# Value features in chunks of whole heads (six of 120 rows for five of 128), with another order of the head of the program and of the last two tiles

## The chip, the cores and the metric

The kernel runs on one core of a Trainium2 chip. The metric is device time in microseconds (us). A core has TensorE (PE) for matrix products into the eight banks of PSUM, VectorE (DVE), ScalarE (ACT) and GpSimd (POOL) for elementwise work, and SyncE (SP), whose queue issues nearly all transfers here.

## The reference, cut to what matters

```python
xn = layernorm(x)                                     # x: 2048 x 640, no scale or shift
q, k, v = split(xn @ wqkv)                            # 32 heads of 20 features
phi = lambda t: where(t > 0, t + 1, exp(t)) + 1e-6
kv  = einsum("bhsd,bhse->bhde", phi(k), v)            # 20 x 20 for each head
z   = einsum("bhsd->bhd", phi(k))
num = einsum("bhqd,bhde->bhqe", phi(q), kv)
den = einsum("bhqd,bhd->bhq", phi(q), z)[..., None] + 1e-6
s   = merge_heads(num / den) @ wo
g   = silu(relu(xn @ w1) @ w2)                        # 640 -> 1728 -> 640
out = x + s * g
```

## The kernel before

The program is a list of operations for each engine, written out by hand in one order. A small scheduler (`Sched`) derives the semaphore waits from the names that each operation reads and writes; each engine then runs its own list strictly in order. So the place of a call in the source sets what stands behind what on an engine, and a transfer that waits holds up those behind it on SP. The 2048 tokens are 16 tiles of 128 (index t), or 4 chunks of 512 (index j); the 640 features are 5 chunks of 128 (C = 5).

*Head.* Tiles 0 to 3 are the way in. For each: `LN_stats` (two halves of statistics and an aggregate on DVE, then the inverse root on POOL), `LN_norm` on DVE, `transposes` (five PE transposes into one bank), `xnT_copy` on ACT, and `K_mm`, ten passes of 320 columns in two banks (key weights from two loads, wk 0 with rows 0 to 383 and wk 1 with the rest). `K_exp` and `K_relu` on ACT empty those banks. `warm(n)` issues n products of the identity into bank 7 that nobody needs. `K_mm(t, b, ks)` with a range does only the row chunks in it. After tile 3 come, for each chunk of 512 tokens, five `Q_block` and thirteen `H_block` (the hidden layer), with statistics, norms, DMA transposes and key products of the next tiles between them.

*Fold.* After the denominators, `G_block` makes GT = xn' phi(k) over all tokens (640 x 640). `kv_block(c, b)` multiplies the value weights of chunk c (128 value features as weight columns) with the columns of GT that belong to the heads of the chunk, 140 or 160 of them, five passes for each chunk; DVE copies the result to `kvp` under a mask `mh` that keeps only each head's own features, since chunks of 128 features cut heads of 20. `kvp` is first filled with zeros by POOL (name `kvz`). `W_block(m)` multiplies `kvp` with `wo` for the 128 key features of block m, over those chunks that hold a head of the block: 2, 3, 3, 3 and 2 chunks, in two halves of 320 columns. So the attention output and its projection become one folded weight `wf` (640 x 640). Each block's two halves are copied by ACT (`wf` columns 0 to 319) and DVE (the rest), and blocks take turns between banks 4, 5 and 6, 7:

```python
        for m in range(C):
            pr[0] = 2 + m % 2
            W_block(m)
```

*Output.* `U(p, hook)` computes the second layer for a pair of tiles, in two groups of 26 passes (L771) with Silu on ACT; `hook` is called between the groups and puts other PE work there: `kv_all` in U(0), `w_all` in U(1), and then `s_tile` for the tiles of an earlier pair. `s_tile` is ten passes of `wf` (L810), then on DVE a product with g (L824), a sum with x (L827) and a store by SP. For the last pair, tiles ea and eb, the kernel before uses `s_half`: one half of each tile ahead of the last group of U(7), the other halves after it, with ea's last sum on POOL and its store issued by ACT.

Of the kernel before, what the change touches and what calls it, by code (L numbers as in the profile page):

```python
# [211 lines left out]
def bass_recurrent_scan__linear_attn_block__dense_activation_relu__prompt_kernel(  # L212
# [25 lines left out]
    x2 = A_x[0]  # L238
    out2 = out[0]

    h_lo = [(P * c) // DH for c in range(C)]
    h_hi = [-(-(P * (c + 1)) // DH) for c in range(C)]

    def cs_of_m(m):
        return [c for c in range(C) if DH * h_lo[c] < P * (m + 1) and DH * h_hi[c] > P * m]

    bf = dt.bfloat16
    f32 = dt.float32
# [10 lines left out]
    NOUT = 4  # L259
    reg3 = nc.alloc_sbuf_tensor("reg3", [P, T * D], bf)  # L260
    pk = reg3[:, :].rearrange("p (t n) -> p t n", t=T)
    kvp = reg3[:, 0:C * D].rearrange("p (c n) -> p c n", c=C)
    outb = reg3[:, C * D:(C + NOUT) * D].rearrange("p (a n) -> p a n", a=NOUT)
    tmpo = reg3[:, (C + NOUT) * D:(C + 2 * NOUT) * D].rearrange("p (a n) -> p a n", a=NOUT)
    pqT = nc.alloc_sbuf_tensor("pqT", [P, C, S], bf)
    hT = nc.alloc_sbuf_tensor("hT", [P, NF, S], bf)
    hTl = nc.alloc_sbuf_tensor("hTl", [P, 2, 512], bf)
# [12 lines left out]

    reg7 = nc.alloc_sbuf_tensor("reg7", [P, XR * D], bf)
    xin = reg7[:, :].rearrange("p (t n) -> p t n", t=XR)
    wo_sb = reg7[:, 0:C * D].rearrange("p (c n) -> p c n", c=C)

    NEK = 4
    NER = 3
# [54 lines left out]
    x_load(1)  # L341
    w_load(wqk[:, 0:KS, D:2 * D], A_wqkv[0:P * KS, D:2 * D], ("wk", 0))
    x_load(2)
    x_load(3)
    w_load(wqk[:, KS:C, D:2 * D], A_wqkv[P * KS:D, D:2 * D], ("wk", 1))

    def late_loads(gate):
        w_load(wqk[:, :, 0:D], A_wqkv[:, 0:D], ("wq",), extra=[gate])
# [18 lines left out]
        sc.group("PE", [(lambda eng: eng.matmul(ps[7][:, 0:P], lhsT=ident[:], rhs=ident[:], start=True, stop=True))  # L367
                        for _ in range(n)], R=[("ident",)], W=[("ps", 7)])

    warm(33)  # L370

    def build_consts():
        sc.op("POOL", lambda eng: eng.memset(mh[:, :, :], 1.0), W=[("mh",)])
# [61 lines left out]
    def K_mm(t, b, ks=None):  # L435
        fns = []
        for a, k in ([(a, k) for a in range(2) for k in range(C)] if ks is None else [(a, k) for k in ks for a in range(2)]):
            if True:
                fns.append(lambda eng, a=a, k=k: eng.matmul(  # L439
                    ps[b + a][:, 0:HN], lhsT=xnT[:, k, tok(t)], rhs=wqk[:, k, D + HN * a:D + HN * (a + 1)],  # L440
                    start=(k == 0), stop=(k == C - 1)))
        wks = [0, 1] if ks is None else sorted({0 if k < KS else 1 for k in ks})
        sc.group("PE", fns, R=[("xnT", t)] + [("wk", i) for i in wks], W=[("ps", b), ("ps", b + 1)])
        if ks is not None:
            sc.allow_unread.update([("ps", b), ("ps", b + 1)])
# [102 lines left out]
    LN_stat(1, 1)  # L548
    LN_aggr(1)
    LN_root_pool(1)  # L550
    LN_stat(2, 0)
    LN_norm(1)
    K_mm(0, 0, range(0, KS))
    transposes(1, 5)
    xnT_copy(1, 5)
    LN_stat(2, 1)
    LN_aggr(2)
    LN_root_pool(2)
    warm(2)
    K_mm(0, 0, range(KS, C))  # L560
    K_exp(0, 0)
    K_relu(0, 0)
    LN_stats(3)
    LN_norm(2)
    K_mm(1, 2, range(0, 4))
    transposes(2, 6)
    xnT_copy(2, 6)
    K_mm(1, 2, range(4, C))
    LN_norm(3)
    warm(3)  # L570
    transposes(3, 4)
    xnT_copy(3, 4)
    K_mm(2, 5)
    K_exp(1, 2)
    K_relu(1, 2)
    K_fin(0)
# [104 lines left out]
    for u in range(2):  # L681
        dma("SP", lambda eng, u=u: eng.dma_start(w2l[64 * u:64 * (u + 1), :], B_w2[NF * P:FF, :]),
            W=[("w2l", u)], extra=[lastW1])
    w_load(wo_sb, A_wo, ("wo",), extra=[last_norm[0]])
    for c in range(C):
        dma("SP", lambda eng, c=c: eng.dma_start(rx[:, c, :], rxd[P * c:P * (c + 1), :]),
            R=[("rxd", i) for i in range(J)], W=[("rx", c)], extra=[lastW1])
# [23 lines left out]
                                                func=ACTF.Copy), R=[("ps", b), ("ps", b + 1)], W=[("GT", k)])  # L711
        return ag

    def kv_block(c, b):
        n0, n1 = DH * h_lo[c], DH * h_hi[c]
        nh = h_hi[c] - h_lo[c]
        sc.group("PE", [(lambda eng, k=k: eng.matmul(ps[b][:, 0:n1 - n0], lhsT=wv_sb[:, k, P * c:P * (c + 1)],  # L717
                                                     rhs=GT[:, k, n0:n1], start=(k == 0), stop=(k == C - 1)))
                        for k in range(C)], R=[("wv",)] + [("GT", k) for k in range(C)], W=[("ps", b)])
        sc.op("DVE", lambda eng: eng.tensor_tensor(  # L720
            out=kvp[:, c, n0:n1].rearrange("p (h e) -> p h e", e=DH),
            in0=ps[b][:, 0:n1 - n0].rearrange("p (h e) -> p h e", e=DH),
            in1=mh[:, c, h_lo[c]:h_hi[c]].unsqueeze(2).to_broadcast([P, nh, DH]), op=ALU.mult),
            R=[("ps", b), ("mh",), ("kvz",)], W=[("kv", c)])

    def W_block(m):
        b = nextp()
        cs = cs_of_m(m)
        fns = []
        for a in range(2):  # L730
            for ci, c in enumerate(cs):
                fns.append(lambda eng, a=a, c=c, ci=ci: eng.matmul(  # L732
                    ps[b + a][:, 0:HN], lhsT=kvp[:, c, P * m:P * (m + 1)], rhs=wo_sb[:, c, HN * a:HN * (a + 1)],
                    start=(ci == 0), stop=(ci == len(cs) - 1)))
        sc.group("PE", fns, R=[("wo",), ("kvz",)] + [("kv", c) for c in cs], W=[("ps", b), ("ps", b + 1)])
        sc.op("ACT", lambda eng: eng.activation(out=wf[:, m, 0:HN], in_=ps[b][:, 0:HN], func=ACTF.Copy),
              R=[("ps", b)], W=[("wf", m, 0)])
        sc.op("DVE", lambda eng: eng.tensor_copy(wf[:, m, HN:D], ps[b + 1][:, 0:HN]),
              R=[("ps", b + 1)], W=[("wf", m, 1)])
# [50 lines left out]

    so = [0]

    def s_half(t, a, b, os_, addE="DVE", dmaE="SP"):
        lo, hi = HN * a, HN * (a + 1)
        sc.group("PE", [(lambda eng, c=c: eng.matmul(  # L795
            ps[b][:, 0:HN], lhsT=pqT[:, c, tok(t)], rhs=wf[:, c, lo:hi], start=(c == 0), stop=(c == C - 1)))
            for c in range(C)], R=[("pqT", t // 4, c) for c in range(C)] + [("wf", c, a) for c in range(C)], W=[("ps", b)])
        sc.op("DVE", lambda eng: eng.tensor_tensor(out=tmpo[:, os_, lo:hi], in0=ps[b][:, 0:HN], in1=g_sb[:, t, lo:hi],  # L798
                                                   op=ALU.mult), R=[("ps", b), ("g", t, a)], W=[("tmpo", os_, lo)])
        sc.op(addE, lambda eng: eng.tensor_tensor(out=outb[:, os_, lo:hi], in0=tmpo[:, os_, lo:hi], in1=xre[:, t, lo:hi],  # L800
                                                  op=ALU.add), R=[("tmpo", os_, lo), ("xre", t // 4)], W=[("outb", os_, lo)])
        dma(dmaE, lambda eng: eng.dma_start(out2[tok(t), lo:hi], outb[:, os_, lo:hi]), R=[("outb", os_, lo)])

    def s_tile(t):
        b = nextp()
        os_ = so[0] % NOUT
        so[0] += 1
        i = t // 4
        for a in range(2):
            sc.group("PE", [(lambda eng, c=c, a=a: eng.matmul(  # L810
                ps[b + a][:, 0:HN], lhsT=pqT[:, c, tok(t)], rhs=wf[:, c, HN * a:HN * (a + 1)],
                start=(c == 0), stop=(c == C - 1))) for c in range(C)],
                R=[("pqT", i, c) for c in range(C)] + [("wf", c, a) for c in range(C)], W=[("ps", b + a)])

        def piece(lo, hi, pin, addE="DVE"):
            shp = "p (a n) -> p a n"
# [13 lines left out]
            dma("SP", lambda eng: eng.dma_start(out2[tok(t), lo:hi], outb[:, os_, lo:hi]), R=kk("outb"))  # L830

        piece(0, D, None)

    gb = [0, 2]
    lastG = None
# [6 lines left out]
            xre[:, 4 * jx:4 * jx + 4, :], x2[512 * jx:512 * (jx + 1), :].rearrange("(t p) n -> p t n", p=P)),  # L842
            W=[("xre", jx)], extra=[lastG])
    def kv_all():
        for c, b in enumerate((0, 1, 2, 3, 0)):
            kv_block(c, b)
        for m in range(2, C):
            divs.append(divide(m))
# [13 lines left out]

    U(0, kv_all)
    U(1, w_all)
    for p in range(2, 7):
        U(p, s_hook(pairs[p - 2], 0 if p % 2 == 0 else 4))
    ea, eb = pairs[7]
    oe = [(so[0] + 4) % NOUT, (so[0] + 5) % NOUT]

    def last_hook():  # L870
        s_hook(pairs[5] + pairs[6], 4)()
        s_half(ea, 0, 0, oe[0])
        s_half(eb, 0, 1, oe[1])

    U(7, last_hook)
    s_half(ea, 1, 4, oe[0], "POOL", "ACT")
    s_half(eb, 1, 5, oe[1])

    sc.wait_all_dma("SP", list(range(nds[0])))

# [30 lines left out]
```

## Time and profile before

| | |
|---|---|
| median of 3 runs | 225.89 us (225.59 to 226.12) |
| the profiled execution, its own time | 225.89 us |
| its span in the profile | 224.2 us |
| PE busy | 218.3 us in 1448 passes |
| DVE, ACT, POOL busy | 102.5, 88.4, 44.6 us |
| value product: 20 passes of 140 columns (L717), five of 160 | 224 and 233 ns each |
| fold: 26 passes of 320 columns (L732) | 299 ns each |
| zero fill of `kvp` (L839) | 2.76 us |

The span goes from the first to the last instruction of the program on the profiled core; the execution's own time is 1.69 us longer. Passes are pipelined, so the duration of one (299 ns) is longer than the distance from one start to the next (136 ns for 320 columns). In the chain of waits each line has a start, a duration and what ran; in the timeline a line has a start, a duration, the engine, the source line, the operation with output and inputs, how many were merged, and in brackets how long the engine had been idle and for whom. PEld is PE's weight load, which overlaps its passes. In the groups, what follows the bar is busy us and mean ns of one. A few PE records are missing from the trace.

### The profile page before, as it was taken

To read this page: it belongs to the slowest core of one execution; us is meant where nothing else is said; L and a number is where in the kernel's file an instruction comes from. 1 tells how busy PE (TensorE), PEld (TensorE's weight loads), DVE (VectorE), ACT (ScalarE), POOL (GpSimd) and SP (SyncE) were. 2 spreads that over 40 slices of the span, in tenths; PEclk is the share of its full clock that TensorE was granted. 3 is DMA by queue.
4 is the path that set the end of the run, shared out by engine and by line. 5 is a ranking of instruction groups with operands and counts; after the bars stand their busy time and mean duration, and the time that the engine had idled before them with its cause. 6 is when DMAs were issued, how large, how long until landed. Compare 5 with 4: busy or idle time off the path is not lost.

```text
span 224.2 us, 3489 instructions
## 1 busy us (share of the span) xinstructions
PE 218.3 (97%) x1448; PEld 135.4 (60%) x1458; DVE 102.5 (46%) x190; ACT 88.4 (39%) x146; POOL 44.6 (20%) x63
## 2 busy tenths in 40 slices
PE   7999999999999999999999999999999999999994
PEld 6764555455554555444477777667767767776772
DVE  4699921796639772967000034540404040431382
ACT  4697765657665666654521112241021103102101
POOL 2437742322541255700000004000000000000001
PEclk9999999999999999999999999999999999999999
DMA  6999910012501150000999999500001010101031
GB/s 180 308 386 288 224 40 0 0 31 59 32 1 29 29 61 1 0 0 3 204 217 294 345 396 320 188 0 3 29 29 54 7 60 3 58 0 61 2 132 42
DMA packets 24239, 23.07 MB, mean 103 GB/s; under 512 B 8992, under 2 KB 23584, under 8 KB 24224
## 3 DMA queue, kind: packets, MB, share of 16 engines
q1 hardware_dynamic: 24080, 22.78, 35.4%
q8 instruction: 11, 0.18, 0.3%
q10 hardware_dynamic: 144, 0.08, 0.1%
q14 instruction: 4, 0.03, 0.1%
HBM read 15.65 MB, written 5.24 MB: 93 GB/s over the span
## 4 chain that ended last, share of the span: by engine, by line
PE 95%; DVE 1%; DMA 1%; issue 1%; ACT 0%
PE psT L771 26%; PE psT L514 25%; PE psT L705 10%; PE psT L491 10%; PE psT L439 10%; PE psT L810 8%; PE psT L732 2%; PE psT L795 1%; PE psT L749 1%; DMA reg<-in_A_x_dram 1%; PE psT L527 1%; PE psT L422 1%; PE psT L717 1%; PE psT L367 1%; DVE stats L383 1%; PE psT L613 1%
## 5 line engine op out<-in xcount | busy, mean ns | idle before, releaser
L771 PE MATMUL psT<-reg,hT 128*128 128x320 bf16 x416 | 58.7, 299 | 0.3
L514 PE MATMUL psT<-reg 128*128 128x512 bf16 x252 | 56.8, 379 | 0.5 <-issue 0.2
L771 PEld LDWEIGHTS psT<-reg,hT 128*128 128x128 bf16 x416 | 40.3, 98 | 17.0 <-PE psT L749 1.6
L514 PEld LDWEIGHTS psT<-reg 128*128 128x128 bf16 x260 | 25.3, 98 | 29.2 <-ACT hT L518 0.4
L767 ACT ACTIVATE reg<-psT 128x640 bf16<-128x640 f32 x16 | 10.8, 702 | 70.1 <-PE psT L749 35.4
L518 ACT ACTIVATE hT<-psT 128x512 bf16<-128x512 f32 x52 | 30.9, 599 | 18.1 <-PE psT L514 17.8
L824 DVE TENSOR_TENSOR reg<-psT,reg 128x640 bf16<-128x640 f32 x14 | 11.6, 825 | 46.0 <-PE psT L810 45.9
L451 POOL TENSOR_TENSOR zacc<-zacc,reg 128x640 f32<-128x640 f32 x16 | 22.6, 1411 | 22.0 <-DVE reg L470 21.7
L439 PE MATMUL psT<-reg 128*128 128x320 bf16 x160 | 24.6, 300 | 0.1
L705 PE MATMUL psT<-reg 128*128 128x320 bf16 x160 | 21.9, 299 | 0.0
L491 PE MATMUL psT<-reg 128*128 128x512 bf16 x98 | 21.8, 379 | 0.1
L439 PEld LDWEIGHTS psT<-reg 128*128 128x128 bf16 x160 | 15.4, 98 | 8.1 <-ACT reg L427 0.4
L810 PE MATMUL psT<-reg,pqT 128*128 128x320 bf16 x140 | 20.0, 299 | 0.0
L705 PEld LDWEIGHTS psT<-reg 128*128 128x128 bf16 x160 | 15.6, 98 | 6.4 <-issue 0.4
L698 DVE TENSOR_TENSOR pqT<-pqT,reg 128x2048 bf16<-128x2048 bf16 x5 | 5.9, 1220 | 27.0 <-DMA reg<-rden_by_feature 26.9
L800 POOL TENSOR_TENSOR reg<-reg 128x320 bf16<-128x320 bf16 x1 | 0.8, 786 | 84.1 <-DVE reg L798 84.1
L810 PEld LDWEIGHTS psT<-reg,pqT 128*128 128x128 bf16 x140 | 13.7, 98 | 5.3
L491 PEld LDWEIGHTS psT<-reg 128*128 128x128 bf16 x100 | 9.8, 98 | 11.2
L383 DVE BATCH_NORM_STATS2 stats<-reg 128x6 f32<-128x320 bf16 x32 | 14.2, 479 | 4.2 <-DMA reg<-in_A_x_dram 4.2
L498 ACT ACTIVATE er<-psT 128x512 bf16<-128x512 f32 x20 | 12.3, 614 | 8.6 <-PE psT L491 3.5
L456 ACT ACTIVATE ek<-psT 128x640 bf16<-128x640 f32 x16 | 11.3, 708 | 9.1 <-PE psT L439 9.1
L468 DVE TENSOR_SCALAR ek<-ek 128x640 bf16<-128x640 bf16 x16 | 5.5, 347 | 18.7 <-ACT ek L456 18.7
(63 smaller groups left out, 159.1 us busy)
## 6 DMA issues: line engine op xcount, KB each, us to landing
reg<-in_A_x_dram SPq DMA_DIRECT2D x16, 160.0 KB, 5.8
rden_by_feature<-rden SPq DMA_DIRECT2D x4, 640.0 KB, 8.7
reg<-rden_by_feature SPq DMA_DIRECT2D x5, 512.0 KB, 11.5
reg<-in_A_x_dram SPq DMA_DIRECT2D x4, 640.0 KB, 7.0
reg<-in_B_w_dram SPq DMA_DIRECT2D x2, 1120.0 KB, 9.8
out_dram<-reg SPq DMA_DIRECT2D x14, 160.0 KB, 1.8
reg<-in_B_w_dram SPq DMA_DIRECT2D x1, 1040.0 KB, 10.1
reg<-in_B_w_dram SPq DMA_DIRECT2D x1, 960.0 KB, 15.0
```

Source lines behind the costliest of these rows:

```text
L383: sc.op("DVE", lambda eng: eng.bn_stats(stats[:, t, a, :], xin[:, t % XR, HN * a:HN * (a + 1)]), R=[("xin", t % XR)], W=[("stats", t, a)])
L439: fns.append(lambda eng, a=a, k=k: eng.matmul(ps[b + a][:, 0:HN], lhsT=xnT[:, k, tok(t)], rhs=wqk[:, k, D + HN * a:D + HN * (a + 1)], star ...
L451: sc.op("POOL", lambda eng: eng.tensor_tensor(out=zacc[:, :], in0=zacc[:, :], in1=pk[:, t, :], op=ALU.add), R=[("zacc",), ("pk", t)], W=[( ...
L456: sc.op("ACT", lambda eng: eng.activation(out=e_.rearrange("p (a n) -> p a n", a=2), in_=ps2(b, HN), func=ACTF.Exp), R=[("ps", b), ("ps", ...
L491: sc.group("PE", [(lambda eng, k=k: eng.matmul(ps[b], lhsT=wqk[:, k, P * f:P * (f + 1)], rhs=xnT[:, k, schunk(j)], start=(k == 0), stop=(k ...
L498: sc.op("ACT", lambda eng: eng.activation(out=e_, in_=ps[b], func=ACTF.Exp), R=[("ps", b)], W=[("er_e", es)])
L514: a = sc.group("PE", [(lambda eng, k=k: eng.matmul(ps[b], lhsT=w1_sb[:, k, P * f:P * (f + 1)], rhs=xnT[:, k, schunk(j)], start=(k == 0), s ...
L518: sc.op("ACT", lambda eng: eng.activation(out=hT[:, f, schunk(j)], in_=ps[b], func=ACTF.Relu), R=[("ps", b)], W=[("hT", j, f)])
L705: fns.append(lambda eng, t=t, a=a: eng.matmul(ps[b + a][:, 0:HN], lhsT=xn[:, t, P * k:P * (k + 1)], rhs=pk[:, t, HN * a:HN * (a + 1)], sta ...
L771: fns = [(lambda eng, u=u, t=t, f=f, n=n: eng.matmul(ps[bs[n] + u][:, 0:HN], lhsT=hT[:, f, tok(t)], rhs=w2_sb[:, f, HN * n:HN * (n + 1)], ...
L810: sc.group("PE", [(lambda eng, c=c, a=a: eng.matmul(ps[b + a][:, 0:HN], lhsT=pqT[:, c, tok(t)], rhs=wf[:, c, HN * a:HN * (a + 1)], start=( ...
L824: sc.op("DVE", lambda eng: eng.tensor_tensor(out=tmpo[:, os_, lo:hi].rearrange(shp, a=na), in0=src, in1=g_sb[:, t, lo:hi].rearrange(shp, a ...
```

## The change

It has three parts.

1. Value features in six chunks of 120 rows, six whole heads each; the fifth chunk holds only two new heads (40 columns) and the sixth starts at row 520. `kv_block` runs six times with 120 weight columns and 120, 120, 120, 120, 40 and 120 columns of GT. Each block of `W_block` then needs two chunks: twenty passes of 120 rows. `kvp` and `wo` have six chunk slots, so the zero fill is longer and `wo` comes in two transfers; the mask of chunk 0 serves for all.
2. In the head, wk 1 is loaded ahead of x3; statistics 2 are finished ahead of norm 1; K 1 runs whole after transposes 2, and the split is on K 2 around transposes 3; exp and relu of K 0 come after the copy of tile 2; warm passes move (33 to 34 at the start, 2 gone, 3 and 3 elsewhere).
3. `s_half` goes. The last two tiles run as `s_tile(t, last=True)` after all of U(7), each half with its own product and sum on DVE and its own store on SP.

```diff
+    VK = (P // DH) * DH
+    NV = -(-D // VK)
+    VR = [min(VK * j, D - VK) for j in range(NV)]
+    VH = [(VR[j] // DH, (VR[j + 1] if j + 1 < NV else D) // DH) for j in range(NV)]
...
     x_load(2)
+    w_load(wqk[:, KS:C, D:2 * D], A_wqkv[P * KS:D, D:2 * D], ("wk", 1))
     x_load(3)
-    w_load(wqk[:, KS:C, D:2 * D], A_wqkv[P * KS:D, D:2 * D], ("wk", 1))
...
-    warm(33)
+    warm(34)
...
-    LN_stat(2, 0)
+    LN_stats(2)
     LN_norm(1)
     K_mm(0, 0, range(0, KS))
     transposes(1, 5)
     xnT_copy(1, 5)
-    LN_stat(2, 1)
-    LN_aggr(2)
-    LN_root_pool(2)
-    warm(2)
     K_mm(0, 0, range(KS, C))
+    LN_norm(2)
+    warm(3)
+    transposes(2, 6)
+    xnT_copy(2, 6)
+    K_mm(1, 2)
     K_exp(0, 0)
     K_relu(0, 0)
     LN_stats(3)
-    LN_norm(2)
-    K_mm(1, 2, range(0, 4))
-    transposes(2, 6)
-    xnT_copy(2, 6)
-    K_mm(1, 2, range(4, C))
     LN_norm(3)
-    warm(3)
+    K_mm(2, 5, range(0, KS))
     transposes(3, 4)
     xnT_copy(3, 4)
-    K_mm(2, 5)
+    K_mm(2, 5, range(KS, C))
+    warm(3)
     K_exp(1, 2)
...
-    w_load(wo_sb, A_wo, ("wo",), extra=[last_norm[0]])
+    dma("SP", lambda eng: eng.dma_start(wo_sb[0:VK, 0:NV - 1, :],
+                                        A_wo[0:VK * (NV - 1), :].rearrange("(c p) n -> p c n", p=VK)),
+        W=[("wo", 0)], extra=[last_norm[0]])
+    dma("SP", lambda eng: eng.dma_start(wo_sb[0:VK, NV - 1, :], A_wo[D - VK:D, :]), W=[("wo", 1)], extra=[last_norm[0]])
...
-        sc.group("PE", [(lambda eng, k=k: eng.matmul(ps[b][:, 0:n1 - n0], lhsT=wv_sb[:, k, P * c:P * (c + 1)],
+        sc.group("PE", [(lambda eng, k=k: eng.matmul(ps[b][0:VK, 0:n1 - n0], lhsT=wv_sb[:, k, r0:r0 + VK],
...
-                    ps[b + a][:, 0:HN], lhsT=kvp[:, c, P * m:P * (m + 1)], rhs=wo_sb[:, c, HN * a:HN * (a + 1)],
+                    ps[b + a][:, 0:HN], lhsT=kvp[0:VK, c, P * m:P * (m + 1)], rhs=wo_sb[0:VK, c, HN * a:HN * (a + 1)],
...
-        for c, b in enumerate((0, 1, 2, 3, 0)):
+        for c, b in enumerate((0, 1, 2, 3, 0, 1)):
             kv_block(c, b)
...
-        piece(0, D, None)
+        if last:
+            piece(0, HN, b)
+            piece(HN, D, b + 1)
+        else:
+            piece(0, D, None)
...
-    def last_hook():
-        s_hook(pairs[5] + pairs[6], 4)()
-        s_half(ea, 0, 0, oe[0])
-        s_half(eb, 0, 1, oe[1])
-
-    U(7, last_hook)
-    s_half(ea, 1, 4, oe[0], "POOL", "ACT")
-    s_half(eb, 1, 5, oe[1])
+    pr[0] = 2
+    for t in pairs[7]:
+        s_tile(t, last=True)
```

More of the change, by code (lines that the diff above doesn't have):

```diff
@@ L239, in bass_recurrent_scan__linear_attn_block__dense_activation_relu__prompt_kernel @@
     out2 = out[0]
[L241 to L245, printed above, removed]
+    VK = (P // DH) * DH
+    NV = -(-D // VK)
+    VR = [min(VK * j, D - VK) for j in range(NV)]
+    VH = [(VR[j] // DH, (VR[j + 1] if j + 1 < NV else D) // DH) for j in range(NV)]
     bf = dt.bfloat16
@@ L261, in bass_recurrent_scan__linear_attn_block__dense_activation_relu__prompt_kernel @@
     pk = reg3[:, :].rearrange("p (t n) -> p t n", t=T)
-    kvp = reg3[:, 0:C * D].rearrange("p (c n) -> p c n", c=C)
-    outb = reg3[:, C * D:(C + NOUT) * D].rearrange("p (a n) -> p a n", a=NOUT)
-    tmpo = reg3[:, (C + NOUT) * D:(C + 2 * NOUT) * D].rearrange("p (a n) -> p a n", a=NOUT)
+    kvp = reg3[:, 0:NV * D].rearrange("p (c n) -> p c n", c=NV)
+    outb = reg3[:, NV * D:(NV + NOUT) * D].rearrange("p (a n) -> p a n", a=NOUT)
+    tmpo = reg3[:, (NV + NOUT) * D:(NV + 2 * NOUT) * D].rearrange("p (a n) -> p a n", a=NOUT)
     pqT = nc.alloc_sbuf_tensor("pqT", [P, C, S], bf)
@@ L282, in bass_recurrent_scan__linear_attn_block__dense_activation_relu__prompt_kernel @@
     xin = reg7[:, :].rearrange("p (t n) -> p t n", t=XR)
-    wo_sb = reg7[:, 0:C * D].rearrange("p (c n) -> p c n", c=C)
+    wo_sb = reg7[:, 0:NV * D].rearrange("p (c n) -> p c n", c=NV)
     NEK = 4
@@ L441, in K_mm @@
                     start=(k == 0), stop=(k == C - 1)))
-        wks = [0, 1] if ks is None else sorted({0 if k < KS else 1 for k in ks})
+        wks = [0, 1] if ks is None else [0 if ks[0] < KS else 1]
         sc.group("PE", fns, R=[("xnT", t)] + [("wk", i) for i in wks], W=[("ps", b), ("ps", b + 1)])
@@ L712, in G_block, with kv_block @@
         return ag
[L714 to L717, printed above, removed]
+    def kv_block(j, b):
+        h0, h1 = VH[j]
+        n0, n1 = DH * h0, DH * h1
+        r0 = VR[j]
+        sc.group("PE", [(lambda eng, k=k: eng.matmul(ps[b][0:VK, 0:n1 - n0], lhsT=wv_sb[:, k, r0:r0 + VK],
                                                      rhs=GT[:, k, n0:n1], start=(k == 0), stop=(k == C - 1)))
@@ L720, in kv_block @@
         sc.op("DVE", lambda eng: eng.tensor_tensor(
[L721 to L724, printed above, removed]
+            out=kvp[0:VK, j, n0:n1].rearrange("p (h e) -> p h e", e=DH),
+            in0=ps[b][0:VK, 0:n1 - n0].rearrange("p (h e) -> p h e", e=DH),
+            in1=mh[0:VK, 0, 0:h1 - h0].unsqueeze(2).to_broadcast([VK, h1 - h0, DH]), op=ALU.mult),
+            R=[("ps", b), ("mh",), ("kvz",)], W=[("kv", j)])
     def W_block(m):
         b = nextp()
-        cs = cs_of_m(m)
+        cs = [j for j in range(NV) if DH * VH[j][0] < P * (m + 1) and DH * VH[j][1] > P * m]
         fns = []
@@ L732, in W_block @@
                 fns.append(lambda eng, a=a, c=c, ci=ci: eng.matmul(
-                    ps[b + a][:, 0:HN], lhsT=kvp[:, c, P * m:P * (m + 1)], rhs=wo_sb[:, c, HN * a:HN * (a + 1)],
+                    ps[b + a][:, 0:HN], lhsT=kvp[0:VK, c, P * m:P * (m + 1)], rhs=wo_sb[0:VK, c, HN * a:HN * (a + 1)],
                     start=(ci == 0), stop=(ci == len(cs) - 1)))
-        sc.group("PE", fns, R=[("wo",), ("kvz",)] + [("kv", c) for c in cs], W=[("ps", b), ("ps", b + 1)])
+        sc.group("PE", fns, R=[("wo", 0), ("wo", 1), ("kvz",)] + [("kv", c) for c in cs], W=[("ps", b), ("ps", b + 1)])
         sc.op("ACT", lambda eng: eng.activation(out=wf[:, m, 0:HN], in_=ps[b][:, 0:HN], func=ACTF.Copy),
@@ L791, in bass_recurrent_scan__linear_attn_block__dense_activation_relu__prompt_kernel, with s_tile @@
     so = [0]
[L793 to L804, printed above, removed]
+    def s_tile(t, last=False):
         b = nextp()
@@ L864, in bass_recurrent_scan__linear_attn_block__dense_activation_relu__prompt_kernel @@
     U(1, w_all)
[L865 to L868, printed above, removed]
-    def last_hook():
-        s_hook(pairs[5] + pairs[6], 4)()
-        s_half(ea, 0, 0, oe[0])
-        s_half(eb, 0, 1, oe[1])
-    U(7, last_hook)
-    s_half(ea, 1, 4, oe[0], "POOL", "ACT")
-    s_half(eb, 1, 5, oe[1])
+    for p in range(2, 8):
+        ts = pairs[p - 2] if p < 7 else pairs[5] + pairs[6]
+        U(p, s_hook(ts, 0 if p % 2 == 0 else 4))
+    pr[0] = 2
+    for t in pairs[7]:
+        s_tile(t, last=True)
     sc.wait_all_dma("SP", list(range(nds[0])))
```

## The prediction

> **What bounds the kernel now.** First I read the page's busy times and its chain of waits by engine, to see whether anything but TensorE counts.
>
> ```profile
> PE 218.3 (97%) x1448; PEld 135.4 (60%) x1458; DVE 102.5 (46%) x190; ACT 88.4 (39%) x146; POOL 44.6 (20%) x63
> PE 95%; DVE 1%; DMA 1%; issue 1%; ACT 0%
> ```
>
> TensorE (PE) is busy for 97% of the span and is 95% of the chain. So each part of the change is worth what it adds to or takes from PE's own sequence, idle gaps included; work elsewhere counts only where PE waits for it. The chain in order of time is nothing but PE from 14.46 to 220.97 us, with "issue" pieces of at most 0.16 us: there is no later wait in which a delay of the first 14 us could vanish. Then I read three stretches. The head, first in the chain (start, duration, what), then in the timeline:
>
> ```profile
> 7.24 0.84 PE psT L439 x6
> 8.08 0.31 PE psT L422 x5
> 8.39 0.02 issue
> 8.42 0.71 ACT reg L427
> 9.13 0.05 issue
> 9.18 1.26 PE psT L439 x8
> ...
> 11.64 2.76 PE psT L439 x20
> ```
>
> ```profile
> 7.44 0.43 DVE L412 TENSOR_SCALAR reg<-reg,mv,rsy 128x640 bf16<-128x640 bf16 x1
> 7.92 0.28 PEld L422 LDWEIGHTS psT<-ident,reg 128*128 128x128 bf16 x5 [0.18 <-DVE reg L412]
> ```
>
> PE waits 0.44 us for one copy of the transposes (L427, 8.42 to 9.12) and otherwise runs; norm 1 starts at 7.44 and transposes 1 follow at 7.92. The fold, from the timeline around 147 us:
>
> ```profile
> 147.70 0.49 DVE L738 CAST reg<-psT 128x320 bf16<-128x320 f32 x1 [4.79 <-PE psT L732]
> 148.30 2.03 PEld L732 LDWEIGHTS psT<-reg 128*128 128x128 bf16 x16 [0.16 <-DVE reg L738]
> ```
>
> The third block's first weight load already waits for VectorE's (DVE's) copy of the first block, since blocks alternate between two bank pairs. The end:
>
> ```profile
> 219.65 0.70 ACT L767 ACTIVATE reg<-psT 128x640 bf16<-128x640 f32 x1 [9.62 <-PE psT L771]
> 220.46 1.04 DVE L798 TENSOR_TENSOR reg<-psT,reg 128x320 bf16<-128x320 f32 x2 [2.82 <-ACT reg L767]
> 221.53 0.47 DVE L800 TENSOR_TENSOR reg<-reg 128x320 bf16<-128x320 bf16 x1
> ```
>
> After PE's last pass DVE has one product and one sum left.
>
> **What the Trainium skill says.** The page "TensorE: Matmul & The Clock Gate", section "Wait — 56ns, not 53.3ns?", gives a warm pass as N/2.4 + about 2.5 ns. The trace agrees: passes of 320 columns start 136 ns apart, of 140 columns 61 ns, transposes of 128 columns 56 ns. Its section "Weight-path perf modes" says that the fast weight load needs the full 128 weight columns. The new value product has 120. The section "LDWEIGHTS (loading the stationary operand)" prices a load at columns/1.2 ns, 100 ns for 120. No run here shows a 120-column load; the nearest rows disagree with that price:
>
> ```profile
> L717 PEld LDWEIGHTS psT<-reg,wv_sb 128*128 128x128 bf16 x25 | 1.6, 98 | 0.1
> L527 PEld LDWEIGHTS psT<-reg 128*64 128x64 bf16 x20 | 1.0, 110 | 1.2 <-ACT hT L518 0.4
> L613 PEld LDWEIGHTS psT<-pqT,zmat 128*32 128x32 bf16 x20 | 0.4, 96 | 0.8 <-issue 0.4
> ```
>
> The trace's operands show loads of 64 and 32 columns in one plain run, 128 columns in four runs of 32. Going from 32 to 64 plain columns adds 14 ns, 0.44 ns a column: 120 columns are estimated at 96 + 88 x 0.44 = 135 ns, of which 120 x 0.44 = 53 ns occupy the load path.
>
> **The head.** Latencies from the timeline: DVE's end to PE's load 0.05 us (7.87 to 7.92), ScalarE's (ACT's) end to PE 0.05, PE's last transpose to ACT 0.04, end of an aggregate to the root on POOL finished 0.97 (8.52 to 9.49), a norm 0.45, two statistics 0.89, five transposes 0.28, a pass 0.136, a copy 0.70. Loads: x2 keeps its place in SP's queue and lands at 7.00; wk1 and x3, landing at 8.23 and 7.41 now, become about 7.8 and 8.2, both ahead of use.
>
> - All of statistics 2 with its aggregate now runs before norm 1. Statistics start at 7.03 when x2 is there; the aggregate starts at 7.95, norm 1 at 8.07 instead of 7.44 and ends at 8.52. Transposes 1: 8.57 instead of 7.92. PE has nothing else to do in these 0.65 us.
> - Transposes 1, then the last four passes of K 0 (0.54) and three warm passes (0.17) end at 9.61. Root 2 is there at 9.13, norm 2 runs 9.16 to 9.60, transposes 2 start at 9.65 and end at 9.95. The copy of transposes 1 (9.07 to 9.77) is over, so K 1 starts at once and ends, 10 x 0.136 later, at 11.31.
> - Statistics 3 queue behind norm 2 on DVE: 9.51 to 10.39, aggregate to 10.63, root 11.60, norm 3 11.63 to 12.08. The first six passes of K 2 (11.31 to 12.12) cover that wait. Transposes 3 from 12.13, four passes of K 2, three warm ones to 13.16. Copy 3 runs 12.62 to 13.33: K 3 starts at 13.38 and its last pass leaves PE free at 14.75.
> - Now the last K pass starts at 14.10 and leaves PE free at 14.24 (Q's first pass, which has no record, fits there). **Head: +0.51 us**, bounds +0.3 and +0.75.
> - The 34th warm pass costs nothing: thirty-three end their issue at 5.11 and transposes 1 of tile 0 wait for norm 0 until 5.35.
> - Behind it, exp and relu of K 0 move past copy 2 on ACT, and ACT and DVE run 0.9 us later until Q. That is covered: the DMA transpose of tile 4, now landing at 22.03, is wanted at 23.95, and the H blocks return to a bank about 3 us after its eviction. x9 to x11 and the DMA transposes are issued up to 0.9 us later on SP, in a queue that moves earlier loads until 20.9.
>
> **The value product.** 25 passes at 61 (five of them 69) ns take 1.56 us. Now there are 30: 25 of 120 columns and 5 of 40. If loads hide, 25 x 52.5 ns = 1.31, and the five short ones are held by their loads at 53: 1.58. I take 54 ns a pass, 1.62: **+0.05**. Bounds: 0 (nothing is saved even with every load hidden), and +1.44 if each pass costs the page's 100 ns (3.0 us). I take the low value since the 64- and 32-column rows show 0.44 ns a column. Six masked copies on DVE in place of five (303 ns each) shift the three later divides by about 0.1 us; their first reader comes after 143 us and after the two early divides. The memset of the padded tile grows from 2.76 us by 3840/3200 to 3.32, ending at 137.45, ahead of the first copy at 137.9. The wo load becomes two DMAs with 900 for 800 KB, so the five loads behind it on SP land 0.3 us later; the first two divides (132.24 to 134.74) move with them, with 3 us to spare, the later three start 2 us after them, and wo itself is needed 16 us after landing.
>
> **The fold.** Thirteen chunk pairs in two halves, 26 passes, become 20: 6 x 0.136 = 0.82 us less. But blocks now take four passes, 0.544 us, and each waits for both copies of the block two before. Block 0 starts at 146.95 and its copies are over at 148.19, whatever is behind it. Block 2 could start at 148.04 but gets its banks only at 148.33, when it starts today as well: the two passes saved in block 1 become idle time. Block 2 ends its issue at 148.87, just when block 1's copies (148.24 to 148.73, plus 0.14) let block 3 start. Block 4 could start at 149.42 and waits for block 2's copies (149.07 to 149.56) until 149.70; it leaves PE free at 150.25, now 150.50. **Fold: -0.25**, bounds -0.15 and -0.82.
>
> **The end.** PE's passes are the same, but the two half tiles that lay ahead of the last 26 passes of U now follow them, so Silu comes 1.36 us earlier, at 218.29 to 219.00. From 219.10 DVE has four pieces to do, each a product (0.49) and a sum, 0.763 us from start to start as at 216.03: they end at 219.10 + 3 x 0.763 + 0.52 + 0.33 = 222.24. Now: 222.00, with one sum on POOL beside. The last transfer then runs without ACT's beside it, 1.6 us as the lone ones now against 1.69. **End: +0.19**, bounds +0.1 and +0.3.
>
> **Sum:** 0.51 + 0.05 - 0.25 + 0.19 = +0.50. The profiled execution took 225.89 us (span 224.2 and 1.69 around it), which is also the median of the runs: 226.4.
>
> **Rivals.**
> - *The fold's saving counts in full* (ends not slower). If the copies of block 0 were over 0.29 us earlier, block 2 could follow at once, and -0.82 would offset the rest: -0.07, 225.8 us. For it: PE is the bound. Against it: the wait at 148.30 and the 0.49 us copy, which the change leaves alone.
> - *Weight loads become the bound in the value product.* At 100 ns a pass, +1.44 instead of +0.05: 227.8 us; each 10 ns above 54 costs 0.3. For it: the page's price and the missing fast load. Against it: 0.44 ns a column in the trace.
> - *The head gives most back.* If norm 1 or copy 3 came some 0.4 us earlier than I place them, the head would cost 0.1 and the sum +0.1: 226.0 us. For it: K 3 waits 0.2 us for copy 3 alone. Against it: norm 1 stands behind 1 us of statistics that cannot start before x2 lands.
>
> **How the numbers follow.** Two tenths of a per cent (0.45 us) is about what a measurement can tell from no change. My forecast gets 0.62, with its own range of 226.1 to 226.7 and about two thirds of it above 226.34; the full fold 0.10; the load bound 0.13; the cheap head 0.15. Slower: two thirds of 0.62, all of 0.13 and a quarter of 0.15, 0.59. Faster: a quarter of the full fold and little else, 0.05. Within: 0.36. The range, 225.9 to 227.3, leaves out the low end of the full fold and the worst of the load bound.
>
> **What would show it.** Transposes 1 at about 8.57, Q's first passes at 14.75 and PE idle of 0.6 us ahead of transposes 1; the 30 value passes in 1.6 us (3 us for the second rival); two gaps of some 0.3 us for DVE's copies in the fold, at its blocks 2 and 4 (none for the first rival); DVE's last sum 1.26 us after PE's last pass instead of 1.03. A fold without gaps, or value passes 60 ns or more apart, would prove the steps wrong.

## The result, and the profile after

| | before | after |
|---|---|---|
| median of 5 runs | 225.72 us (225.59 to 226.12) | 226.70 us (226.44 to 227.03) |
| ratio, with its 95% interval | | 1.0041 [1.0026, 1.0055] |
| the profiled execution, and its span | 225.89, 224.2 us | 226.44, 224.7 us |
| PE's last pass ends | 220.97 us | 220.99 us |
| from there to the end of the execution's time | 4.92 us | 5.45 us |

The change costs 0.93 us by the ratio (0.6 to 1.2), where +0.50 was forecast. The last two rows say where to look: in these two profiles PE ends its work at the same time, since the fold gives back what the head loses (with x2 landing 0.35 us earlier in the second one), and half a microsecond lies behind PE's last pass. Lines in the changed kernel are numbered otherwise: the value product is L718, its masked copy L721, the fold L733 with DVE's copy L739, the zero fill L833, the output's passes L800 and its product and sum L814 and L817.

The head, first in the chain of waits (start, duration, what), then in the timeline (with the idle time and whom it was for):

```profile
2.18 4.47 DMA reg<-in_A_x_dram
6.65 0.02 issue
6.67 0.90 DVE stats L383 x2
7.57 0.02 issue
7.59 0.22 DVE mv L387
7.81 0.08 issue
7.89 0.31 POOL rsv L391
8.20 0.07 issue
8.27 0.58 POOL rsy L393
8.86 0.03 issue
8.88 0.46 DVE reg L412
9.34 0.05 issue
9.39 0.45 PE psT L422 x5
9.84 2.17 PE psT L439 x16
```

```profile
7.72 0.40 DVE L412 TENSOR_SCALAR reg<-reg,mv,rsy 128x640 bf16<-128x640 bf16 x1
...
8.16 0.28 PEld L422 LDWEIGHTS psT<-ident,reg 128*128 128x128 bf16 x5 [0.31 <-DVE reg L412]
...
8.88 0.45 DVE L412 TENSOR_SCALAR reg<-reg,mv,rsy 128x640 bf16<-128x640 bf16 x1 [0.77 <-POOL rsy L393]
```

The chain no longer runs through PE here. It goes from x2's landing through statistics 2, their root on POOL and norm 2 to transposes 2. Norm 1 started at 7.72, later than before, and is not on it. The value product and the fold, from the groups kept apart by shape:

```profile
L718 PEld LDWEIGHTS psT<-reg,wv_sb 128*120 128x120 bf16 x30 | 1.8, 135 | 0.0
L718 PE MATMUL psT<-reg,wv_sb 128*120 128x120 bf16 x25 | 1.7, 219 | 0.0
L718 PE MATMUL psT<-reg,wv_sb 128*120 128x40 bf16 x5 | 0.4, 204 | 0.0
L833 POOL MEMSET reg<- 128x3840 bf16 x1 | 3.3, 3297 | 38.6 <-PE psT L705 38.6
```

and the fold in the timeline:

```profile
147.28 3.40 PE L733 MATMUL psT<-reg 120*128 120x320 bf16 x20
...
148.63 0.94 PEld L733 LDWEIGHTS psT<-reg 120*128 120x128 bf16 x8 [0.43 <-DVE reg L739]
...
149.95 0.40 PEld L733 LDWEIGHTS psT<-reg 120*128 120x128 bf16 x4 [0.38 <-DVE reg L739]
```

The weight load of 120 columns takes 135 ns, and the loads follow each other every 55 ns, for passes of 120 and of 40 columns alike (all 30 passes took 1.65 us, the 25 of before 1.56). In the fold the loads of blocks 2 and 4 wait for DVE's copies; PE starts block 2 0.29 us and block 4 0.24 us after it could have. The end, from the timeline:

```profile
218.31 0.70 ACT L768 ACTIVATE reg<-psT 128x640 bf16<-128x640 f32 x1 [8.26 <-PE psT L772]
219.12 0.49 DVE L814 TENSOR_TENSOR reg<-psT,reg 128x320 bf16<-128x320 f32 x1 [2.98 <-ACT reg L768]
...
221.41 0.48 DVE L814 TENSOR_TENSOR reg<-psT,reg 128x320 bf16<-128x320 f32 x1
221.93 0.33 DVE L817 TENSOR_TENSOR reg<-reg 128x320 bf16<-128x320 bf16 x1
```

DVE works from 219.12 to 222.26 with no gap above 0.04 us.

### The profile page after: what moved, and what is told of

It is laid out like the page before. It is cut to its first block, busy times and chain, and to the rows that moved or that the text cites. A ratio compares the mean times of both kernels' runs of the same rounds, so it can differ in the third digit from the quotient of the medians.

```text
span 224.7 us, 3494 instructions
## 1 busy us (share of the span) xinstructions
PE 218.2 (97%) x1449; PEld 135.1 (60%) x1459; DVE 102.6 (46%) x192; ACT 88.3 (39%) x146; POOL 44.3 (20%) x62
## 4 chain that ended last, share of the span: by engine, by line
PE 92%; DMA 2%; DVE 2%; issue 1%; ACT 1%; SPq 1%; POOL 0%; DVEq 0%
PE psT L772 25%; PE psT L514 25%; PE psT L705 10%; PE psT L491 10%; PE psT L439 9%; PE psT L800 8%; DMA reg<-in_A_x_dram 2%; PE psT L733 1%; PE psT L750 1%; PE psT L527 1%; DVE reg L814 1%; PE psT L718 1%; PE psT L610 1%; DVE reg L817 0%; DVE stats L383 0%
## 5 line engine op out<-in xcount | busy, mean ns | idle before, releaser
L814 DVE TENSOR_TENSOR reg<-psT,reg 128x640 bf16<-128x640 f32 (+1 forms) x18 | 13.5, 750 | 49.0 <-PE psT L800 46.0
L800 PE MATMUL psT<-reg,pqT 128*128 128x320 bf16 x160 | 22.9, 299 | 0.0
L800 PEld LDWEIGHTS psT<-reg,pqT 128*128 128x128 bf16 x160 | 15.7, 98 | 6.1
L508 DVE SCALAR_TENSOR_TENSOR pqT<-er 128x512 bf16<-128x512 bf16 x15 | 12.9, 860 | 0.5
```

What stands on the lines that cost most here:

```text
L508: sc.op("DVE", lambda eng: eng.scalar_tensor_tensor(out=pqT[:, f, schunk(j)], in0=e_, scalar=1.0, in1=r_, op0=ALU.min, op1=ALU.add), R=[(" ...
L800: sc.group("PE", [(lambda eng, c=c, a=a: eng.matmul(ps[b + a][:, 0:HN], lhsT=pqT[:, c, tok(t)], rhs=wf[:, c, HN * a:HN * (a + 1)], start=( ...
```

## The experiments

My theory was the prediction's sum: a late head, two gaps in the fold, four pieces on DVE at the end. What the sum missed was open. Each kernel was timed beside the one before on one chip; "us" from a ratio is that ratio of 225.8.

**Part 2 alone.** Before with the head's edits: the order of wk 1 and x3, statistics, K 1, K 2 and warm passes. Its core:

```diff
+    LN_stats(2)
     LN_norm(1)
...
+    LN_norm(2)
+    warm(3)
+    transposes(2, 6)
+    xnT_copy(2, 6)
+    K_mm(1, 2)
...
+    K_mm(2, 5, range(0, KS))
     transposes(3, 4)
     xnT_copy(3, 4)
+    K_mm(2, 5, range(KS, C))
```

> Before with part 2 alone (loads, statistics 2 ahead of norm 1, order of K 1 and K 2, warm passes). My theory: tile 2's landing starts statistics 2, and norm 1, transposes 1 and all behind follow; with x2 at 7.0 us K 3 ends 0.5 us later than before, with x2 at 6.65 as in the profile of after 0.25 us later. So +0.5 us in the median of the runs and between +0.2 and +0.6 in the profile, following x2's landing one to one. Rival (the profile of after is typical): +0.25 us in all runs.

1.0021 [1.0012, 1.0030], +0.47 us. The profile had x2 at 6.23 and the last K pass at 13.94, earlier than before's 14.10. Half a microsecond in the runs was expected. That the profile would be 0.2 to 0.6 us slower was not met, since this execution took 225.74 us with an early x2; counted from x2's landing, the last K pass came 0.61 us later than before (7.71 us for 7.10).

**Part 3 alone.** Before with the last pair as whole tiles:

```diff
-    U(7, last_hook)
-    s_half(ea, 1, 4, oe[0], "POOL", "ACT")
-    s_half(eb, 1, 5, oe[1])
+    pr[0] = 2
+    for t in pairs[7]:
+        s_tile(t, last=True)
```

> Before with part 3 alone (last two tiles after all of U, four pieces on DVE and four stores on SP). My theory: DVE's last sum ends 0.25 us later after PE's last pass than before, the last store lands 0.16 us later, and SP needs 0.34 us more from its last wait to its closing drain, as in the profile of after: +0.5 us. Rival (the slow closing drain was chance): +0.2 us.

1.0001 [0.9992, 1.0011], +0.02 us (-0.2 to +0.25). In its profile DVE's last sum ends 1.26 us after PE's last pass (before 1.03), the last store lands 2.88 us after it (before 2.75), and the execution ends 5.08 us after it (before 4.92): +0.16. SP's closing drain (the last but one instruction of its list) follows its last branch after 0.11 us, as before. The rival was right: the slow drain does not come with part 3 alone. SP does pause for 0.35 us more than before, but behind the drain, where the other engines have ended already.

**Part 1 alone.** Before with the six chunks (value product, mask, fold, zero fill and the two wo transfers), nothing else:

```diff
-        for c, b in enumerate((0, 1, 2, 3, 0)):
+        for c, b in enumerate((0, 1, 2, 3, 0, 1)):
             kv_block(c, b)
```

> Before with part 1 alone (six chunks of 120 rows; head and end as before). My theory: 30 value passes at 55 ns, +0.08 us, and two gaps of 0.24 to 0.29 us at blocks 2 and 4 of the fold, so 26 passes become 20 but only 0.31 us is saved: together -0.2 us against before. Rival (the saving counts in full): no gaps, -0.7 us. Second rival (the 120-row load of wo, which held up the loads behind it by 2.3 us in the profile of after, costs time): 0 or slower than before.

1.0012 [0.9992, 1.0033]. The profile fits my theory: from the last K pass's start to the end of PE's last pass it takes 206.65 us, before 206.87, -0.22. The runs do not: most lie at 225.2 to 226.0, four of 14 at 226.9 to 227.7, where the highest of 51 runs of before was 226.58. That is what the second rival expected: something in part 1 costs time in some executions.

**Part 1 with the fold spread.** The blocks of the fold put between the passes of U(1)'s second group:

```diff
+                for i, w in enumerate(between):
+                    sc.group("PE", fns[5 * i:5 * i + 5], R=Rh, W=bk(n))
+                    w()
+                sc.group("PE", fns[5 * len(between):], R=Rh, W=bk(n))
```

> Part 1 alone, with the five blocks of the fold spread into the second group of 26 passes of U(1): five passes of U ahead of each block. Same passes in all. My theory: a block's banks are free again while U's passes run, the two gaps (0.53 us in the profile of after) go, and it is 0.4 to 0.5 us faster than part 1 alone, 0.65 us faster than before. Rival (the gaps are not from the copies but from 120-row weight loads or from the chunks themselves): same as part 1 alone.

1.0015 [0.9997, 1.0033], five of 14 runs late in the same way: as a time it settles nothing. But its profiled execution, 227.5 us, was one of the late ones, and its chain shows the cause in that execution:

```profile
124.10 14.56 DMA reg<-rden_by_feature
138.66 0.02 issue
138.68 0.03 DVE pqT L701
138.72 1.11 issue
139.83 0.29 DVE reg L724
140.11 0.04 issue
140.16 0.76 PE psT L721 x10
```

Five loads of `rden` follow wo on SP: the inverses of the denominators by feature, with which the five divides on DVE multiply. The one for the second divide landed at 138.66. The two early divides (L701) ran from 137.39 to 139.91, and the masked copies of the value product (L724) stand behind them on DVE, so PE's last ten value passes (L721) waited until 140.16 for a free bank. The waits of three kernels show how late the first rden load landed; the longest idle time of DVE ends there:

```profile
DVE pqT L698 <- DMA reg<-rden_by_feature: 26.9, 1, 26.9
```

before, then after, then this one:

```profile
DVE pqT L698 <- DMA reg<-rden_by_feature: 29.0, 1, 29.0
```

```profile
DVE pqT L701 <- DMA reg<-rden_by_feature: 31.7, 1, 31.7
```

It landed at 132.2, 134.6 and 137.4. Ahead of it on SP stands `wo`: 800 KB in five chunks of 128 rows landed 2.1 us after the load before it, 750 KB in five chunks of 120 rows 3.6 us (after), 4.8 (part 1 alone) and 4.3 (this one), and the sixth chunk another 0.4 to 0.6. Here the load before it was late as well, by 2.6 us against before. A stretch of before with wo in flight, then one of after (the last three figures are the granted clock, the busy share of the DMA engines and GB/s):

```profile
128.90:130.90 2.00, 2.00 (x17) 1.45 (x15) 0.00 (x0) 0.70 (x1) 0.00 (x0) 1.00 1.03 401
129.40:132.90 3.50, 3.50 (x28) 2.54 (x26) 0.00 (x0) 0.70 (x1) 0.00 (x0) 1.00 1.07 259
```

The single packets of the traces show that the loads next to wo are slowed too. From 125 to 130 us a packet of 1280 bytes (a row of wo or of w2) took 98 to 102 ns in the three profiles with 120-row chunks in this place and 67 to 69 in the five with before's wo; a packet of 4096 bytes (a row of the rden loads) took 275 to 281 for 165 to 167.

**wo behind the rden loads.** One edit, made to part 1 alone and to after:

```diff
-    dma("SP", lambda eng: eng.dma_start(wo_sb[0:VK, 0:NV - 1, :],
-                                        A_wo[0:VK * (NV - 1), :].rearrange("(c p) n -> p c n", p=VK)),
-        W=[("wo", 0)], extra=[last_norm[0]])
-    dma("SP", lambda eng: eng.dma_start(wo_sb[0:VK, NV - 1, :], A_wo[D - VK:D, :]), W=[("wo", 1)], extra=[last_norm[0]])
     for c in range(C):
         dma("SP", lambda eng, c=c: eng.dma_start(rx[:, c, :], rxd[P * c:P * (c + 1), :]),
             R=[("rxd", i) for i in range(J)], W=[("rx", c)], extra=[lastW1])
+    dma("SP", lambda eng: eng.dma_start(wo_sb[0:VK, 0:NV - 1, :],
+                                        A_wo[0:VK * (NV - 1), :].rearrange("(c p) n -> p c n", p=VK)),
+        W=[("wo", 0)], extra=[last_norm[0]])
+    dma("SP", lambda eng: eng.dma_start(wo_sb[0:VK, NV - 1, :], A_wo[D - VK:D, :]), W=[("wo", 1)], extra=[last_norm[0]])
```

> Part 1 alone, wo issued behind the rden loads. My theory: the runs at 226.4 to 227.7 of part 1 alone go, all lie within 0.8 us, and the median is 0.2 us below before (0.08 us lost in the value product, 0.31 gained in the fold). Rival (the late runs of part 1 alone come from something else, such as the longer zero fill): the spread stays at 2.5 us.

0.9987 [0.9980, 0.9994], -0.29 us; all 18 runs between 225.2 and 226.0. The late runs, nine of 28 in the two versions before it, are gone, and the gain of part 1 stands.

```profile
130.37 2.51 DVE L701 TENSOR_TENSOR pqT<-pqT,reg 128x2048 bf16<-128x2048 bf16 x2 [25.36 <-DMA reg<-rden_by_feature]
```

The early divides now end at 132.88, more than four microseconds ahead of the first masked copy.

> After with one change: the two wo transfers are issued behind the five rden loads on SP, not ahead of them. My theory: the 120-row wo transfer (3.6 to 4.8 us instead of 2.1) holds up the rden loads, and in the slower executions the two early divides push the value copies on DVE, and PE waits. Then the first divide starts near 131 us instead of 134.6, and the runs keep the head's half us but lose their upper part: median 226.2, none above 226.7. Rival (the transfer is always hidden in after): same as after, 226.7.

1.0034 [1.0022, 1.0046], median 226.55, three of 8 runs above 226.7. This is a miss: the first divide came early as expected (129.85), but the time fell by 0.16 us and the two intervals overlap. So it is not shown that the late transfer costs anything in the whole change, and the runs above 226.7 stay unexplained. What the profiles show is behind PE: 5.47 us from its last pass to the end here, 5.45 in after, 5.08 in part 3 alone, 4.92 to 4.97 in all kernels that keep `s_half`. Of the 0.37 us over part 3 alone, 0.34 lie in one place: from SP's last branch to its closing drain it takes 0.45 us in both, 0.11 to 0.14 in all others.

The traces say more of this pause when SP's instructions are counted (the timeline leaves out the ones that are no transfers). It goes by the place in SP's list. The four kernels with 79 recorded instructions on SP (before and the three that change the head alone) have no pause. In the seven with 80 (six versions of part 1, and part 3 alone) SP reaches its last instruction, the 80th, 0.47 to 0.49 us after the drain, for 0.14 to 0.15. With both parts there are 81, since each adds a transfer, and the drain is now the 80th: it comes 0.34 us late, and the last instructions of the other engines, which follow it, come late with it. In the one kernel with 84 (the next one) the 80th waits for a store, and no pause is seen. So neither part pays for the pause alone, and the two together do. What SP waits for is not shown, and no run changed the count by itself.

**wo in transfers of 128 rows,** in the old place on SP:

```diff
+    for c in range(NV - 1):
+        dma("SP", lambda eng, c=c: eng.dma_start(wo_sb[:, c, :], A_wo[VK * c:VK * c + P, :]),
+            W=[("wo", c)], extra=[last_norm[0]])
```

> Part 1 alone, wo in its old place on SP, but chunks 0 to 4 loaded as five transfers of 128 rows (eight rows of each are not used) and the last as one of 120. My theory: the number of rows sets the speed, so chunks 0 to 4 land within about 2.1 us of w2 instead of 3.6 to 4.8, the last one 0.6 us later, and the late runs of part 1 alone go nearly all. Rival (bytes or the second transfer set it): wo lands as late as in part 1 alone and the spread stays.

0.9990 [0.9982, 0.9999], -0.23 us, 13 of 14 runs at 225.91 or below. The five chunks landed 2.5 us after the load before them, the last one 0.6 later, and a packet of 1280 bytes took 72 ns. With the late runs of part 1 alone (4 of 14) gone, this fits the slow transfer as their cause. It does not fit in full: in this profile the first rden load landed at 134.19, about as late as in after, in part because the load ahead of wo was late too (by 1.2 us against before), and the second divide ended 0.84 us ahead of the first masked copy. This edit also made five transfers of one; but before and part 1 move the five chunks in the same form, one transfer each, and differ in the rows. Why 120 rows are slower stays open, and a single chunk of 120 rows took no more than 0.6 us.

**Spread fold, wo late.**

> Part 1 alone, blocks of the fold spread into U(1)'s second group, wo issued behind the rden loads. My theory: no gap in the fold and no late divides, so 0.08 us lost and 0.82 gained, less about 0.1 for the split groups: 0.6 to 0.7 us faster than before, 225.1 us, and faster than part 1 with wo late by 0.4 us. Rival (gaps go but come back elsewhere, the later Silu for instance): same as part 1 with wo late.

1.0000 [0.9992, 1.0009]: a miss, 0.3 us slower than the unspread one. The chain names the new wait:

```profile
152.96 0.56 PE psT L736 x4
153.51 0.02 issue
153.54 0.51 DVE reg L742
154.04 0.08 issue
154.12 3.69 PE psT L775 x26
```

With five passes ahead of each block only one of the 26 is left behind the last. U(2) takes the banks of that block (4 and 5) and now waits for its copies: PE's next pass starts 0.65 us late, more than the two gaps that went.

**Spread fold with cover at its end, wo late.** Block 0 first, then 4, 4, 4, 5 and 9 passes of U behind the blocks:

```diff
+                for w, ni in zip(between, (4, 4, 4, 5, 9)):
+                    w()
+                    sc.group("PE", fns[i0:i0 + ni], R=Rh, W=bk(n))
+                    i0 += ni
```

> As the version with spread blocks and wo late, but block 0 first and 4, 4, 4, 5 and 9 passes of U after the five blocks, so that nine passes (1.22 us) cover the last block's copies ahead of U(2), where that version had one pass and a gap of 0.65 us. My theory: no gap left, 0.6 us faster than that version, 0.6 us faster than before, 225.2 us. Rival (the split groups cost what the gaps did): no faster than part 1 with wo late (0.28 us below before).

0.9970 [0.9957, 0.9982], -0.68 us, median 225.01. From the last K pass's start to PE's end it takes 206.15 us: 0.72 less than before, 0.50 less than part 1 with its gaps. That is the size of the two gaps (0.53) and confirms what they were.

**Norm 1 in the head, two ways.** The prediction's first step alone, in before, and its reverse in part 2:

```diff
-    LN_stat(2, 0)
+    LN_stats(2)
     LN_norm(1)
```

> Before with one edit of the head: all of statistics 2 with aggregate and root ahead of norm 1 (the first step of the prediction alone). First theory (norm 1's delay carries through): norm 1 starts 1.07 us after x2 lands instead of 0.44, the last K pass 6.66 us after norm 1 as in the profiles of before, so +0.6 us where x2 binds, +0.5 in the median. Second theory (PE's order of K 1 and K 2 is what costs in part 2): 0 to +0.2 us.

1.0023 [1.0013, 1.0033], +0.52 us: the first theory. This one step, whose other lines (second half, aggregate and root of tile 2) only move up, costs as much as all of part 2.

```diff
-    LN_stats(2)
+    LN_stat(2, 0)
     LN_norm(1)
+    LN_stat(2, 1)
+    LN_aggr(2)
+    LN_root_pool(2)
```

> Part 2 alone, but norm 1 ahead of the second half of statistics 2, as before. First theory: norm 1 is 0.63 us earlier and all of part 2's loss goes, 0 against before. Second theory (in part 2's order norm 2 and its root are the path, since K 1 stands whole behind transposes 2, and statistics 3 behind norm 2): norm 2 starts 2.5 us after x2 instead of 2.23 and everything behind it is later, +0.7 us against before, slower than part 2 alone by 0.2 to 0.3.

1.0036 [1.0024, 1.0049], +0.81 us: the second theory. Norm 1 starts early and the kernel is slower. From its timeline and then that of part 2 alone:

```profile
8.91 0.45 DVE L412 TENSOR_SCALAR reg<-reg,mv,rsy 128x640 bf16<-128x640 bf16 x1 [1.01 <-POOL rsy L393]
9.41 0.28 PEld L422 LDWEIGHTS psT<-ident,reg 128*128 128x128 bf16 x5 [0.58 <-DVE reg L412]
```

```profile
8.47 0.45 DVE L412 TENSOR_SCALAR reg<-reg,mv,rsy 128x640 bf16<-128x640 bf16 x1 [0.78 <-POOL rsy L393]
8.97 0.28 PEld L422 LDWEIGHTS psT<-ident,reg 128*128 128x128 bf16 x5 [0.23 <-DVE reg L412]
```

Both lines are norm 2 and transposes 2, with x2 landing at 6.26 and 6.23. Norm 2 is 0.44 us later when norm 1 stands ahead of its statistics, and so is the last K pass. Some 0.12 us of it is a wait of norm 1 for its own root, which ended at 6.79 here. In the runs the difference to part 2 alone is 0.34 us, with intervals that overlap.

**x2 ahead of wk 0,** on top of the spread fold:

```diff
+    x_load(2)
     w_load(wqk[:, 0:KS, D:2 * D], A_wqkv[0:P * KS, D:2 * D], ("wk", 0))
-    x_load(2)
```

> As the one before it, with x2 loaded ahead of wk 0. My theory: the median execution of before waits for x2 (landing 6.2 to 7.4 in the profiles, the last K pass following it one to one above 6.7); with x2 there at about 4, norm 1 starts at root 1, at 6.95, the upper half of the runs comes down, and the median falls by another 0.1 to 0.3 us. Rival (wk 0, now landing where x2 did, takes over the wait at the first K pass): no change or up to 0.3 us slower.

0.9957 [0.9946, 0.9969], -0.97 us, median 224.87, the highest of 6 runs 225.24. This is the fastest version, ahead of both kernels. It is 0.3 us below the one without the edit, though those two intervals overlap, so a gain by this edit is not shown. x2 landed at 5.2, not at 4, and the last K pass started at 13.78. Three other profiles with before's head have it at 13.77, with x2 at 6.32 and 6.67. In all four the chain runs not through x2 but through ACT (its table load, then the copy of tile 0): an earlier x2 gains nothing below that.

x2 explains most of the profiles' differences in the head (us, from the traces; the last column is the last K pass minus x2's landing). Of the seven left out, four fit (7.10 with before's head, 7.70 with part 2's) and three do not: the two with x2 at 5.21 and 6.32 just named, which x2 no longer holds up, and part 1 alone, where PE's first six K passes were slower (1.06 us for 0.84):

| kernel | x2 lands | norm 1 starts | last K pass starts | difference |
|---|---|---|---|---|
| before | 7.00 | 7.44 | 14.10 | 7.10 |
| part 3 alone (head as before) | 6.67 | 7.10 | 13.77 | 7.10 |
| spread with cover (head as before) | 7.42 | 7.85 | 14.51 | 7.09 |
| statistics 2 first | 6.84 | 7.91 | 14.54 | 7.70 |
| after | 6.65 | 7.72 | 14.35 | 7.70 |
| part 2 alone | 6.23 | 7.30 | 13.94 | 7.71 |
| part 2, norm 1 ahead | 6.26 | 6.82 | 14.38 | 8.12 |

## Why the prediction was right or wrong, point by point

- **Right: PE's sequence is the bound, and a delay of the head is kept.** PE's time from the last K pass to its end is 206.87 or 206.88 us in the five kernels with before's fold, whatever the head did.
- **The head, +0.51: size right, and the path only half seen.** Predicted was a last K pass 7.6 us after x2 lands; it was 7.70, before 7.10: +0.60 at the same landing, +0.47 in the runs of part 2 alone. The profile of after shows only +0.25, since its x2 came 0.35 us earlier; its transposes 1 started 1.51 us after x2, where 1.57 were placed. The steps from norm 2 to K 3 were placed right, but norm 1 was named first and made the hinge of the third rival. In part 2's order the path is statistics 2, root 2, norm 2, and behind it K 1. Moving norm 1 ahead of the second half of statistics 2 gave nothing back (+0.81 for +0.47). So in this order the third rival's premise, that an earlier norm 1 gives most back, is wrong.
- **The value product, +0.05: right,** +0.08. The load took the 135 ns that were read off the rows of 64 and 32 columns, not the page's 100, and the loads overlap: 55 ns a pass, where 54 were taken. So the price that the Trainium skill states in "TensorE: Matmul & The Clock Gate", section "LDWEIGHTS (loading the stationary operand)", columns/1.2 ns, was neither the load's duration here nor the spacing, and the second rival falls.
- **The wo load, "0.3 us later": this step failed.** The first rden load landed 2.4 us later in after and 5.2 in the spread version. I took bytes over the rate of the transfer before, 900 for 800 KB, and called 3 us a cover without asking how firm either number was. In after's profile one microsecond of cover was left, in the late execution of the spread version none. It cost part 1 alone its gain in the mean of the runs (+0.27 us, and -0.29 with wo late). In the whole change no cost of it is shown.
- **The fold, -0.25: right in size and mechanism.** 20 passes took 3.24 us for 3.55, -0.31, with gaps of 0.29 and 0.24 where 0.29 and 0.28 were placed. The first rival falls: nearly all of its 0.82 us comes (0.72 with the value product's 0.08 against it) only where other passes stand in the gaps.
- **The end, +0.19: right for part 3 (+0.16 in the profile, within the runs' interval), mis-sized for the whole,** +0.53. The prediction's own two figures, 0.24 us for DVE and 0.09 back for the last transfer, come to +0.15. The term left out is 0.34 us between SP's last branch and its closing drain, the largest error of the sum. It appeared there in both profiles of kernels with all three parts and in none of the other twelve, where the pause falls behind the drain or is not seen. The count of SP's instructions tells the place in all fourteen; what SP does in that time is not shown.
- **The sum.** By its parts now: +0.47 (head), -0.23 (value product and fold), +0.16 (end), +0.34 (the drain) make +0.74, inside the measured interval of 0.6 to 1.2. The late wo transfer would bring it to +0.90, near the measured +0.93, if the 0.16 us between the two ratios were its cost; that is argued, since the intervals with and without the wo edit overlap. That the median of 226.70 us still lies in the forecast range is owed to the width of the range: the forecast had no term for the pause and too small a one for the transfer.

## What to carry to other kernels

Fewer passes are worth their time only if the banks that they free are free in time: look at which copy the next block waits for, and fill the gap with independent passes, some of them behind the last block as well. When a load changes its shape, do not take its rate from the old shape, and look at everything queued behind it, down to the engine order in which its readers stand ahead of others. Before comparing two profiles of a head, line them up on the transfer that it waits for; one execution's landing can hide half a microsecond. And what neither of two parts costs alone they can cost together, as SP's pause does here.

## What the runs showed of the hardware that I had not expected

- 750 KB in one transfer of five chunks of 120 rows took 3.6 to 4.8 us where 800 KB in chunks of 128 rows took 2.1. In the profile's stretches the sixteen DMA engines were busy throughout in both, but moved 259 GB/s against 401, and single packets of 1280 bytes took 98 to 102 ns for 67 to 69, those of the loads around it too. The Trainium skill, "DMA: Bandwidth & Descriptors", section "Why a DMA increments its semaphore by 16 and not by 1", says that a transfer uses the largest number of engines up to 16 that divides the slowest dimension of both its sides, 15 for 120 rows. An estimate from this is 7% (16/15), not 70% and more; no row here shows how many engines a transfer used.
- x2's landing lay between 6.2 and 7.4 us in the profiles of the kernels that load it in the same place, and from about 6.7 us on the last K pass of before's head followed it one to one.
- Weight loads of 120 columns (135 ns each) follow each other every 55 ns, whether the passes between them have 120 or 40 columns.
- SP's pause of 0.34 us ahead of the 80th instruction of its list moves the time of the whole kernel when that is the drain (two of fourteen profiles), and not when it is the last one behind the drain (seven).
